# The decay sums of a forgetting attention as three float16 parts in two tiles, with new ranks for the planner

## The chip, the cores and the metric

The kernel runs on one core of one Trainium2 chip. The time is the device time of one execution in microseconds (us), from launch to end. The core has a matrix engine (TensorE: PE for its products, PEld for its weight loads), a vector engine (VectorE, DVE), an engine for functions of one input (ScalarE, ACT), a slower general engine (GpSimd, POOL), and a queue that issues DMA transfers (SyncE, SP). Each works through its own instructions in order; semaphores tie them together.

## The reference

Three layers in a row, all in float32. Only the attention is touched by the change.

```python
# B, H, S, D = 4, 8, 576, 64: 32 heads
scores = (1.0 / sqrt(D)) * (q @ k.T)
log_f = log(clip(f, 1e-4, 1.0))              # f: [B, H, S]
cum = cumsum(log_f, axis=-1)
scores = where(causal, -1e9, scores + cum[..., :, None] - cum[..., None, :])
attn = exp(scores - max(scores)); attn = attn / (sum(attn) + 1e-9)
x = attn @ v                                  # joined to [B, S, 512]
# token mixing over S (576 -> 256 -> 576), then channel mixing (512 -> 1536 -> 512)
u = x + (relu(x.T @ w_tok1) @ w_tok2).T
x = u + relu(u @ w_ch1) @ w_ch2
# gated layer: 512 -> 1024, a convolution of three taps over S, a sigmoid gate, 1024 -> 512
h = conv(relu(x @ w_in), conv_w); out = (h_in * sigmoid(h)) @ w_out
```

The softmax of a row is the same when a constant is added to it, so the term of the row (`cum[:, None]`) can be left out: the kernel adds only the column's term, the decay, to the scores.

## The kernel before, in words

The 32 heads are worked off in 16 pairs. One load `load_qk` brings q and k of a pair, one head in partitions 0 to 63 and the other in 64 to 127. `score` (L862 on) makes the scores of a pair in three sets of row blocks: block 4 (576 columns wide, two banks), blocks 0 and 3, blocks 1 and 2. A set is four products of q and k for the two heads (L885), and then two or four *decay products* (L889): a column of `sel`, repeated 128 times, selects the rows of `dec` that belong to the head and adds its decay to every row of the scores.

`smax` (DVE, L903) masks the scores and takes the row maximum, `sexp` (ACT, L909) the exponentials. Heads 0 to 7 and the last two are transposed by PE (`ptr`, L942), the others by a DMA, for which POOL makes a float16 high part and DVE a low part (`lo_part`, L924). `pv` multiplies by v (L974 in float32 for heads 0 to 7, L979 to L981 in float16 later). Four heads are a group; `t1` and `t2` mix the tokens of a group (`mm3`, L276 to L278; `t2_x`, L1119, transposes x). After two groups, u of a batch is scaled (`u_scale`), split into float16 high and low parts (`u_part`, low part at L508), and the first five blocks of the channel mixing can run (`channel_mix`: `m1` reads uh and ul, `rl` at L561 is its DVE part). These float16 products are the only large work of PE that needs no softmax, and they fill its gaps from then on.

Weights arrive packed; ACT (L313) and DVE (L317, L318) decode them, and DVE makes their low parts (L469, below called weight low part).

The decays come first of all. Four DMAs (L706) bring the whole of f, 32 rows, to each quarter of the partitions; DVE clips it (L712), ACT takes the logarithm (L713), DVE sums it (L714), and the sums are written as a rounded part and a remainder, two rows of fp32r per head, in both halves of the partitions (L718, L721). ACT copies pieces of `dec` to where the sets of blocks need them (L723).

What follows is put in order by a planner, the class `Order`. Every step is a task `T(engine, cost, rank, function, ...)` with the keys it reads and writes. The planner keeps a clock of its own and on each engine takes the task that can begin first, at equal times the one of lowest rank; the instructions are then emitted in that order, and each engine keeps it. So ranks, costs and the spacing of the heads (`PER`) set the order and nothing else. `SETR` and `LATER` are offsets of the ranks of the channel weights; `LATE` puts the channel products behind everything else.

## Time and profile before

| | |
|---|---|
| time, median of 3 runs | 727.55 us (725.85 to 730.85) |
| profiled execution | 727.58 us; span from first to last instruction 725.8 us |
| busy, share of the span | PE 97%, PEld 79%, DVE 69%, ACT 58%, POOL 30% |
| mean granted clock of TensorE | 0.988 |
| chain that ended last | PE 81%, DVE 7%, issue 6%, POOL 4% |

The span has 1.8 us around it that the profile doesn't show. A share of busy time is a mean over stages, and a matmul's record is longer than the time that it takes from the next one, because matmuls are pipelined. So PE at 97% says that PE nearly always has something in flight, not that it streams all the time; the stretches must be read one by one.

### The profile page before, as it was taken

The numbers are of one execution on the slowest core, as the hardware profiler recorded it, in microseconds if no ns is written. First come the engines' busy times: TensorE is split into PE (matmuls) and PEld (weight loads), VectorE is DVE, ScalarE is ACT, GpSimd is POOL, SyncE is SP. The second block draws the span as 40 slices with busy tenths as digits, with TensorE's granted clock in tenths as the row PEclk, the third lists the DMA queues.
The fourth block names the chain that finished last, engine by engine and source line by source line (L and its number), as shares of the span: only waits on it lengthen the run. The fifth ranks groups of instructions, "written<-read, shape, count | busy, mean of one in ns | idle before, by whom it ended". The sixth has DMA issues, their size and how long they took to land.

```text
span 725.8 us, 16282 instructions
## 1 busy us (share of the span) xinstructions
PE 706.5 (97%) x6412; PEld 573.8 (79%) x6412; DVE 502.8 (69%) x1225; ACT 420.8 (58%) x924; POOL 214.8 (30%) x270
## 2 busy tenths in 40 slices
...
GB/s 210 152 126 171 178 223 205 212 179 285 216 222 171 159 133 185 220 264 140 158 184 117 247 157 162 100 131 137 67 60 58 50 58 35 58 18 25 34 34 34
DMA packets 149581, 101.13 MB, mean 139 GB/s; under 512 B 86592, under 2 KB 141632, under 8 KB 149504
## 3 DMA queue, kind: packets, MB, share of 16 engines
...
q14 instruction: 27, 0.22, 0.1%
...
## 4 chain that ended last, share of the span: by engine, by line
PE 81%; DVE 7%; issue 6%; POOL 4%; ACT 1%; DMA 0%; SPq 0%; POOLq 0%; DVEq 0%; ACTq 0%
PE w L276 14%; PE w L277 14%; PE w L278 14%; PE z L277 7%; PE z L278 7%; PE z L276 7%; PE z L885 6%; PE w L974 3%; PE w L942 2%; POOL g L271 2%; PE z L889 2%; DVE pl L924 1%; PE w L1119 1%; PE w L980 1%; PE w L979 1%
## 5 line engine op out<-in xcount | busy, mean ns | idle before, releaser
L276 PEld LDWEIGHTS <-w 128*128 128x128 f16 x1280 | 125.4, 98 | 36.0 <-issue 4.5
L278 PEld LDWEIGHTS <-w 128*128 128x128 f16 x1280 | 125.5, 98 | 33.0 <-issue 1.1
L277 PEld LDWEIGHTS <-w 128*128 128x128 f16 x1280 | 125.3, 98 | 32.1 <-issue 1.1
L276 PE MATMUL w<-uh,w 128*128 128x288 f16 x416 | 119.8, 288 | 0.0
L278 PE MATMUL w<-uh,w 128*128 128x288 f16 x416 | 119.6, 288 | 0.0
L277 PE MATMUL w<-ul,w 128*128 128x288 f16 x416 | 119.6, 288 | 0.0
L1385 DVE SCALAR_TENSOR_TENSOR cv<-hp,cw,cv 128x286 f32<-128x286 f32 (+1 forms) x128 | 75.1, 593 | 43.4 <-ACT cv L1379 41.1
L271 POOL TENSOR_TENSOR g<-sg,g 128x286 f16<-128x286 f32 (+1 forms) x64 | 54.9, 863 | 156.1 <-ACT g L265 154.4
L909 ACT ACTIVATE t<-t,m 128x576 f32<-128x576 f32 (+4 forms) x160 | 81.7, 554 | 20.9 <-DVE m L903 18.5
L557 ACT ACTIVATE r<-w 128x288 f16<-128x288 f32 x96 | 39.0, 406 | 87.2 <-PE w L278 86.8
L903 DVE CUSTOM_DVE_ANT_0 t<-z,mask 128x576 f32<-128x576 f32 (+4 forms) x160 | 70.5, 479 | 17.9 <-PE z L889 17.8
L277 PE MATMUL z<-g,w 128*128 128x286 f16 (+1 forms) x256 | 73.3, 286 | 0.7 <-POOL g L271 0.7
L276 PE MATMUL z<-g,w 128*128 128x286 f16 (+1 forms) x256 | 73.0, 285 | 1.0 <-ACT g L265 1.0
L561 DVE SCALAR_TENSOR_TENSOR r<-w,r 128x288 f16<-128x288 f32 x96 | 43.4, 453 | 43.4 <-ACT r L557 43.2
L278 PE MATMUL z<-g,w 128*128 128x286 f16 (+1 forms) x256 | 72.9, 285 | 0.0
L634 POOL TENSOR_TENSOR p<-p,u 128x288 f32<-128x288 f32 x32 | 25.5, 828 | 152.1 <-DMA p<-p_d 151.3
L885 PE MATMUL z<-qk 64*128 64x288 f32 (+4 forms) x384 | 61.8, 432 | 7.0 <-DVE m L903 3.9
L271 POOL TENSOR_TENSOR xl<-xf,xh 128x320 fp32r<-128x320 f32 x32 | 34.0, 1064 | 110.2 <-ACT xh L265 110.1
L276 PE MATMUL w<-vh,w 128*128 128x288 f16 x224 | 64.1, 286 | 0.0
L277 PE MATMUL w<-vl,w 128*128 128x288 f16 x224 | 64.1, 286 | 0.0
L278 PE MATMUL w<-vh,w 128*128 128x288 f16 x224 | 64.1, 286 | 0.0
L276 PE MATMUL z<-r,w 128*128 128x288 f16 x224 | 64.1, 286 | 0.0
...
## 6 DMA issues: line engine op xcount, KB each, us to landing
...
qk<-in_qk_dram SPq DMA_DIRECT2D x16, 608.0 KB, 4.9
...
```

Source lines behind the costliest of these rows:

```text
L271: nc.gpsimd.tensor_tensor(o, a, b, ALU.subtract)
L276: nc.tensor.matmul(ps, wh, xh, start=(first and i == 0), stop=False)
L277: nc.tensor.matmul(ps, wh, xl, start=False, stop=False)
L278: nc.tensor.matmul(ps, wl, xh, start=False, stop=(last and i == n - 1))
L557: nc.scalar.activation(out=t[:, 0, :], in_=box["z", m], func=AF.Relu)
L561: nc.vector.scalar_tensor_tensor(t[:, 1, :], box["z", m], 0.0, f32(t[:, 0, :]), ALU.max, ALU.subtract)
L634: nc.gpsimd.tensor_tensor(box["p"][:, d], box["p"][:, d], box["u"][:, d], ALU.add)
L885: nc.tensor.matmul(out_[x], t[r, Q0[i]:Q0[i] + 128], t[r, k0:k0 + n], start=first, stop=False)
L903: nc.vector.tensor_tensor_reduce(to, z_t.pop((n, i)), mk, -0.125, 3e38, ALU.add, ALU.min, m_t[n][0:rows, i:i + 1])
L909: nc.scalar.activation(out=tt[0:rows, o:o + w], in_=tt[0:rows, o:o + w], func=AF.Exp, bias=m_t[n][0:rows, i:i + 1], scale=-1.0)
L974: nc.tensor.matmul(o[:, 0:65], p32(n)[:, 128 * blk:128 * blk + 128], vp32_t[g % 2][:, slot, hh, :], start=(j == 0), stop=(j == nb - 1))
L1385: nc.vector.scalar_tensor_tensor(cv, hp_t[m][:, s0 + t:s1 + t], cw[:, t, m:m + 1], cv, ALU.mult, ALU.add)
```

## The change

- **Parts.** The sum is written as three float16 parts in three rows of their own; with 16 heads to a tile there are two tiles, `dec_t[0]` for heads 0 to 15 and `dec_t[1]` for heads 16 to 31. Row r of a half holds part r // 16 of head r % 16. `less` is a column of -1 and 0 that subtracts the parts already written, so that each of the three needs the same four DVE instructions over all 128 partitions (`decay_parts`). `sel` has 16 columns, and both tiles use it.
- **Loads.** f comes by two DMAs, one to a tile, each repeating 16 rows eight times. The load of the first q and k stands between them.
- **Tables.** ACT fetches the table of the logarithm with a dummy instruction ahead of the data, and that of the exponential with another one directly after the two logarithms.
- **Second tile.** Its sum, parts and copies are planner tasks.
- **Numbers of the planner.** Costs, `PER`, `SETR`, `LATER` and the spacing of weights are changed.

```diff
@@ -204,9 +204,9 @@
     FULL = 2 * HG
     BY_PE = [n < FULL or n >= NH - 2 for n in range(NH)]
 
-    SETR = ((-5.0, 30.0),)
-    LATER = (-10.0, 20.0, 40.0)
-    PER = 6.0
+    SETR = ((5.0, 20.0),)
+    LATER = (-30.0, 20.0, 40.0)
+    PER = 6.5
 
     const = ctx.enter_context(tc.tile_pool(name="const", bufs=1))
     work = ctx.enter_context(tc.tile_pool(name="work", bufs=1))
@@ -469,7 +469,7 @@
                 nc.vector.scalar_tensor_tensor(t[:, 512:1024], WT[i], pw[:, 0:1], t[:, 0:512], ALU.mult, ALU.subtract)
 
             T("ACT", 0.75, cranks[k], high, reads=[("W", i), ("pw", name), *opened(j)], writes=[("W", j)])
-            T("DVE", 0.75, cranks[k], low, reads=[("W", i), ("pw", name)], writes=[("W", j)])
+            T("DVE", 1.0, cranks[k], low, reads=[("W", i), ("pw", name)], writes=[("W", j)])
         return pw
 
 
@@ -674,9 +674,10 @@
 
 
         DEC4, DEC12 = 128, S + 128
-        dec = ap1.tile([128, DEC12 + 512], F32R, name="dec", bufs=1)
-        dmain = dec[:, 64:64 + S]
-        sel = ap1.tile([128, NH], F32R, name="sel", bufs=1)
+        HB = NH // 2
+        dec_t = [ap1.tile([128, DEC12 + 512], F16, name=f"dec{a}", bufs=1) for a in range(2)]
+        sel = ap1.tile([128, HB], F16, name="sel", bufs=1)
+        less = ap1.tile([128, 2], F32, name="less", bufs=1)
 
         nc.gpsimd.memset(mask[:, 0:128], 0.0)
         warm = bank("z")
@@ -701,32 +702,58 @@
             v_t[g] = t
 
 
-        ft = ap1.tile([128, S], F32, tag="xh", name="ft")
-        for a in range(4):
-            nc.sync.dma_start(ft[NH * a:NH * a + NH], f)
-        load_qk(0)
-        zer = ap1.tile([128, S], F32, tag="xl", name="zer")
-        cum = ap1.tile([128, S], F32, tag="us", name="cum", bufs=2)
+
+
+
+        nc.vector.memset(ones, 1.0)
+        tiny = ap1.tile([128, 1], F32, name="tiny", bufs=1)
+        nc.scalar.activation(out=tiny, in_=ones, func=AF.Ln)
+        ft_t = [ap1.tile([128, S], F32, tag="xh", name="ft"), None]
+        cum_t = [ap1.tile([128, S], F32, tag="us", name="cum", bufs=2) for _ in range(2)]
+        ft_t[1] = cum_t[1]
+        for a in range(2):
+            nc.sync.dma_start(ft_t[a], f[HB * a:HB * a + HB].partition_broadcast(128 // HB))
+            if a == 0:
+                load_qk(0)
+        zer = ap1.tile([128, 1], F32, name="zer", bufs=1)
+        part = [ap1.tile([128, S], F16, tag="t1h", name="part"), ap1.tile([128, S], F16, tag="t1l", name="part")]
         nc.vector.memset(zer, 0.0)
         make_identity(nc, ident)
-        nc.vector.tensor_scalar(ft, ft, 1e-4, 1.0, ALU.max, ALU.min)
-        nc.scalar.activation(out=ft, in_=ft, func=AF.Ln)
-        nc.vector.tensor_tensor_scan(cum, ft, zer, 0.0, ALU.add, ALU.add)
-        for a in range(4):
-            r = slice(NH * a, NH * a + NH)
-            nc.vector.tensor_copy(sel[r], ident[r, NH * a:NH * a + NH])
-        nc.scalar.activation(out=dmain, in_=cum, func=AF.Copy, scale=-8.0)
-        for a in (1, 3):
-            r = slice(NH * a, NH * a + NH)
-            nc.vector.scalar_tensor_tensor(dmain[r], cum[r], -8.0, f32(dmain[r]), ALU.mult, ALU.subtract)
-        for a, n in ((DEC12 - 64, 64), (0, 64), (DEC12, WD[1]), (DEC12 + WD[1], WD[2])):
-            nc.scalar.activation(out=dec[:, a:a + n], in_=f32(dmain[:, 0:n]), func=AF.Copy)
+        own = ident.rearrange("p (x k h) -> p x k h", x=2, k=4)
+        nc.vector.tensor_reduce(less[:, 0:1], own[:, :, 0], mybir.AxisListType.XY, ALU.add)
+        nc.vector.tensor_scalar(less[:, 0:1], less[:, 0:1], 1.0, None, ALU.subtract)
+        nc.vector.tensor_reduce(less[:, 1:2], own[:, :, 2], mybir.AxisListType.XY, ALU.add, negate=True)
+        for a in range(2):
+            nc.vector.tensor_scalar(ft_t[a], ft_t[a], 1e-4, 1.0, ALU.max, ALU.min)
+            nc.scalar.activation(out=ft_t[a], in_=ft_t[a], func=AF.Ln)
+        nc.scalar.activation(out=tiny, in_=ones, func=AF.Exp)
+
+        def decay_sum(a):
+            nc.vector.tensor_tensor_scan(cum_t[a], ft_t[a], zer.to_broadcast([128, S]), 0.0, ALU.add, ALU.add)
+
+        def decay_parts(a):
+            cum, main = cum_t[a], dec_t[a][:, 64:64 + S]
+            nc.vector.tensor_copy(part[a], cum)
+            nc.vector.scalar_tensor_tensor(cum, part[a], less[:, 0:1], cum, ALU.mult, ALU.add)
+            nc.vector.tensor_copy(part[a], cum)
+            nc.vector.scalar_tensor_tensor(main, part[a], less[:, 1:2], cum, ALU.mult, ALU.add)
+
+        def decay_copies(a):
+            for at, n in ((DEC12 - 64, 64), (0, 64), (DEC12, WD[1]), (DEC12 + WD[1], WD[2])):
+                nc.scalar.activation(out=dec_t[a][:, at:at + n], in_=dec_t[a][:, 64:64 + n], func=AF.Copy)
+
+        decay_sum(0)
+        one = ap1.tile([128, HB], F32, name="one", bufs=1)
+        nc.vector.tensor_reduce(one, ident.rearrange("p (x k h) -> p h x k", x=2, k=4)[:, :, :, 0:3],
+                                mybir.AxisListType.XY, ALU.add)
+        nc.vector.tensor_scalar(sel, one, -8.0, None, ALU.mult)
+        decay_parts(0)
+        decay_copies(0)
 
         nc.gpsimd.memset(mask[:, 128:704], 0.0)
         nc.gpsimd.affine_select(
             out=mask[:, 512:640], in_=mask[:, 512:640], pattern=[[-1, 128]],
             compare_op=ALU.is_ge, fill=-8e9, base=0, channel_multiplier=1)
-        nc.vector.memset(ones, 1.0)
 
         TB = 4
         t_t = [ap2.tile([128, PW], F32, tag=f"t{i}", name=f"t{i}", bufs=1) for i in range(TB)]
@@ -885,8 +912,8 @@
                     nc.tensor.matmul(out_[x], t[r, Q0[i]:Q0[i] + 128], t[r, k0:k0 + n], start=first, stop=False)
             for out_, k0, n in sums:
                 for x, r in enumerate(halves):
-                    h = 2 * p + x
-                    nc.tensor.matmul(out_[x], sel[r, h:h + 1].to_broadcast([64, 128]), dec[r, k0:k0 + n],
+                    a, h = divmod(2 * p + x, HB)
+                    nc.tensor.matmul(out_[x], sel[r, h:h + 1].to_broadcast([64, 128]), dec_t[a][r, k0:k0 + n],
                                      start=False, stop=True)
 
         def smax(n, i):
@@ -1015,7 +1042,7 @@
         def x_lo(n):
             pool_sub(x_part(n, "xl"), x_of(n), f32(x_part(n, "xh")))
 
-        PE_S = {(4,): 1.42, (0, 3): 1.33, (1, 2): 1.28}
+        PE_S = {(4,): 1.45, (0, 3): 1.35, (1, 2): 1.2}
         DVE_S = {4: 0.81, 3: 0.69, 2: 0.56, 1: 0.42, 0: 0.29}
         ACT_E = {4: 0.78, 3: 0.67, 2: 0.56, 1: 0.46, 0: 0.34}
         SEG = ((4, 3), (2, 1, 0))
@@ -1028,7 +1055,7 @@
                 T("SP", 0.4, t0 - 9, load_qk, p, writes=[kq], moved=2.6, pools=A2)
             for blocks in SETS:
                 kz = [turn("z") for _ in range(2 if blocks == (4,) else 1)]
-                T("PE", PE_S[blocks], t0 + 1, score, p, blocks, reads=[kq], writes=[*kz, ("scores",)], pools=A2 + A1,
+                T("PE", PE_S[blocks], t0 + 1, score, p, blocks, reads=[kq] + [("dec", 1)] * (p >= HB // 2), writes=[*kz, ("scores",)], pools=A2 + A1,
                   ring=kz)
                 for x, i in ((x, i) for x in range(2) for i in blocks[::-1]):
                     n = 2 * p + x
@@ -1057,7 +1084,7 @@
                           writes=[("ptl", n % 2, a)], pools=A2 + ["a3"], ring=[kw])
                 else:
                     for q in range(2):
-                        T("POOL", (1.15, 0.8)[q], rank + 4, hi_part, n, q, reads=[(*kt, i) for i in SEG[q]],
+                        T("POOL", (1.22, 1.05)[q], rank + 4, hi_part, n, q, reads=[(*kt, i) for i in SEG[q]],
                           writes=[("ph", n % 2, q)], pools=A2)
                     T("SP", 1.5, rank + 5, transp, n, 0, reads=[("ph", n % 2, 0), ("ph", n % 2, 1)],
                       writes=[("pth", n % 2, a) for a in range(len(QUADS))], moved=2.5, pools=A3)
@@ -1075,7 +1102,7 @@
                 T("DVE", 0.5, rank + 6, norm, n, reads=[kw] + ([] if n < FULL else [("vsc", g % 3)]), writes=[("rs", n % 2)], pools=A1, ring=[kw])
                 T("DVE", 0.46, rank + 6, xout, n, reads=[kw, ("rs", n % 2)], writes=[("xf", g % 2, n % HG)], pools=A1, ring=[kw])
                 T("ACT", 0.45, rank + 6, x_hi, n, reads=[("xf", g % 2, n % HG)], writes=[("xh", n % HG)], pools=A1)
-                T("POOL", 0.9, rank + 6, x_lo, n, reads=[("xf", g % 2, n % HG), ("xh", n % HG)],
+                T("POOL", 1.05, rank + 6, x_lo, n, reads=[("xf", g % 2, n % HG), ("xh", n % HG)],
                   writes=[("xl", n % HG)], pools=A1)
 
 
@@ -1168,7 +1195,7 @@
                 kw = turn("w")
                 T("PE", 1.8, t0 + 3, t1, g, a, reads=[*xk, *W1K], pools=A1, ring=[kw],
                   writes=[kw, ("t1h", a), ("t1l", a)])
-                T("ACT", 0.37, t0 + 3, t1_hi, g, a, reads=[kw], writes=[("t1h", a)], pools=A1, ring=[kw])
+                T("ACT", 0.37, t0 + 3, t1_hi, g, a, reads=[kw, ("dec", 1)], writes=[("t1h", a)], pools=A1, ring=[kw])
                 T("DVE", 0.42, t0 + 3, t1_lo, g, a, reads=[kw, ("t1h", a)], writes=[("t1l", a)], pools=A1, ring=[kw])
             uk = [("us", g % 2, d, e) for d in range(NDM) for e in range(2)]
             for d in range(NDM):
@@ -1177,7 +1204,7 @@
                     first = d == 0 and e == 0
                     T("PE", 1.42, t0 + 4, t2, g, d, e, writes=[kw, *(uk if first else [("us", g % 2, d, e)])], pools=A1, ring=[kw],
                       reads=[(x, a) for x in ("t1h", "t1l") for a in range(KT)] + W2K + xf)
-                    T("ACT", 0.4, t0 + 4, u_copy, g, d, e, reads=[kw], writes=[("us", g % 2, d, e)], pools=A1, ring=[kw])
+                    T("ACT", 0.4, t0 + 4, u_copy, g, d, e, reads=[kw, ("dec", 1)], writes=[("us", g % 2, d, e)], pools=A1, ring=[kw])
             T("SP", 0.4, t0 + 5, u_out, g, reads=uk, writes=[("u_d", 2 * b, half), ("u_d", 2 * b + 1, half)],
               moved=2.4, pools=A1)
             T("DVE", 1.3, t0 + 4, u_largest, g, reads=uk, writes=[("um", b, half)], pools=A1)
@@ -1218,7 +1245,10 @@
         W1K = [("tokw", k) for k in range(3)]
         W2K = [("tokw", k) for k in range(3, 7)]
         v_tasks(0, -8)
-        AVAIL = [(H * (b + 1) - 1) * PER + 30 for b in range(B)]
+        T("DVE", 1.4, 16, decay_sum, 1, writes=[("dec", 1)], pools=["a1"])
+        T("DVE", 2.6, 22, decay_parts, 1, writes=[("dec", 1)], pools=["a1"])
+        T("ACT", 1.0, 24, decay_copies, 1, writes=[("dec", 1)], pools=["a1"])
+        AVAIL = [(H * (b + 1) - 1) * PER + 35 for b in range(B)]
         LATE = 1000.0
         for k, (block, hi, lo) in enumerate(tok_w):
             weight(block, lambda hi=hi, lo=lo: (hi, lo), 10 + 5.0 * k, ("tokw", k), pools_=["a1"])
@@ -1231,7 +1261,7 @@
                 q = t0 + SETR[x][y]
                 pw = weight_set(f"c{y + 1}{x}", [(name, m, (col_block if y == 0 else row_block)(w, m)) for m in ms],
                                 list(range(at, at + n)), at - 1 if at else 2 * M1,
-                                [q + 2.5 * k for k in range(n)], [q + 2.5 * n + 2.5 * k for k in range(n)], factor)
+                                [q + 2.0 * k for k in range(n)], [q + 2.0 * n + 2.0 * k for k in range(n)], factor)
                 if y == 0:
                     pws.append([pw])
                 else:
```

Where a name moved: L885, L889, L903 and L909 of before are L912, L916, L930 and L936 after the change; `mm3` keeps its lines.

Three places show how the order moves. The first is the beginning of DVE. `ft` (and in the changed kernel `cum`, for the second tile) holds f, L712 or L727 clips it, L714 or L732 sums it, L721 or L736 to L739 write the parts, and L903 or L930 is the first row maximum, of head 0. Before:

```order
L710 MEMSET zer 128x576
L712 TENSOR_SCALAR ft<-ft 128x576
L714 SCALAR_TENSOR_TENSOR cum<-ft,zer 128x576
L717 CAST sel<-ident 32x32 x4
L721 SCALAR_TENSOR_TENSOR dec<-cum,dec 32x576 x2
L729 MEMSET ones 128x1
L903 ISA t_182,m<-z,mask 128x576
```

Now:

```order
L727 TENSOR_SCALAR ft<-ft 128x576
L727 TENSOR_SCALAR cum<-cum 128x576
L732 SCALAR_TENSOR_TENSOR cum<-ft,zer 128x576
L747 TENSOR_REDUCE one<-ident 128x16
L749 TENSOR_SCALAR sel<-one 128x16
L736 CAST part<-cum 128x576
L737 SCALAR_TENSOR_TENSOR cum<-part,less,cum 128x576
L738 CAST part<-cum 128x576
L739 SCALAR_TENSOR_TENSOR dec_133<-part,less,cum 128x576
L732 SCALAR_TENSOR_TENSOR cum<-cum,zer 128x576
...
L930 ISA t_193,m<-z,mask 128x576
```

The clip of the second tile stands ahead of the first sum, and the second tile's sum and its four parts (the rows left out) stand ahead of head 0's maximum.

The second place is PE ahead of the scores of pair 4 (heads 8 and 9). L974 or L1001 is `pv` in float32, L1119 or L1146 the transposes of x for `t2`, L942 or L969 transposes attention weights. Before:

```order
L974 MATMUL w<-vp_195,pt 128x65 x10
L885 MATMUL z<-qk_148 128x288 x4
L889 MATMUL z<-dec,sel 128x288 x4
L1119 MATMUL w<-ident,xf 128x128 x3
L276 MATMUL w<-w2h,t1h 128x288
L277 MATMUL w<-w2l,t1h 128x288
L278 MATMUL w<-w2h,t1l 128x288
...
L942 MATMUL w<-ident,t_184 128x128 x12
```

Now:

```order
L1146 MATMUL w<-ident,xf 128x128 x3
L276 MATMUL w<-w2h,t1h 128x288
L277 MATMUL w<-w2l,t1h 128x288
L278 MATMUL w<-w2h,t1l 128x288
...
L1001 MATMUL w<-vp_206,pt 128x65 x15
L969 MATMUL w<-ident,t_195 128x128 x12
L912 MATMUL z<-qk_150 128x288 x4
```

Three transposes of x, the six products of `t2` that follow them, and twelve transposes of attention weights moved from behind the first scores of pair 4 to ahead of them.

The third place is DVE between heads 11 and 12, where the channel mixing of the first batch begins: `r<-w,r` is `rl` (L561), `ul` a low part of u (L508), L317 and L318 decode a weight. Before:

```order
L508 SCALAR_TENSOR_TENSOR ul<-us,su_73,uh 128x576 x3
L924 SCALAR_TENSOR_TENSOR pl<-t_185,ph 128x640
L561 SCALAR_TENSOR_TENSOR r<-w,r 128x288
L903 ISA t_182,m<-z,mask 128x576
...
L318 SCALAR_TENSOR_TENSOR w_119<-w_119,wraw 128x512
```

Now:

```order
L561 SCALAR_TENSOR_TENSOR r<-w,r 128x288 x2
L930 ISA t_196,m<-z,mask 128x192
...
L318 SCALAR_TENSOR_TENSOR w_120<-w_120,wraw 128x512
L561 SCALAR_TENSOR_TENSOR r<-w,r 128x288
L951 SCALAR_TENSOR_TENSOR pl<-t_196,ph 128x1024
L951 SCALAR_TENSOR_TENSOR pl<-t_196,ph 128x640
L561 SCALAR_TENSOR_TENSOR r<-w,r 128x288
L317 TENSOR_SCALAR wraw<-wraw 128x512
L318 SCALAR_TENSOR_TENSOR w_121<-w_121,wraw 128x512
L561 SCALAR_TENSOR_TENSOR r<-w,r 128x288 x2
L930 ISA t_193,m<-z,mask 128x576
```

Six `rl` stand ahead of head 12's first maximum (the last row) where there was one.

## Rows read from the trace of the kernel before

**Rows 1.** Windows, cut at the first 128x576 maximum of heads 2, 8, 14 and 24.

```profile
core 0: us, PE busy (x) PEld busy (x) DVE busy (x) ACT busy (x) POOL busy (x), PEclk, DMA share, GB/s
20.40:69.60 49.20, 49.20 (x406) 43.10 (x406) 32.62 (x109) 38.87 (x86) 18.25 (x23) 1.00 0.46 146
69.60:132.00 62.40, 55.41 (x534) 45.31 (x533) 57.80 (x145) 41.33 (x88) 34.08 (x34) 0.92 0.83 192
132.00:216.10 84.10, 83.20 (x922) 67.42 (x920) 76.37 (x209) 57.78 (x121) 45.74 (x43) 1.00 0.98 228
```

**Rows 2.** Windows of the stretches at half clock, and of a late one.

```profile
10.00:16.80 6.80, 5.83 (x24) 3.54 (x25) 2.90 (x11) 5.22 (x11) 0.72 (x1) 0.50 1.19 256
88.50:91.90 3.40, 3.40 (x18) 3.40 (x17) 3.37 (x9) 2.82 (x4) 1.87 (x3) 0.50 1.13 208
105.60:112.40 6.80, 5.80 (x24) 3.81 (x25) 6.80 (x10) 4.74 (x10) 4.29 (x3) 0.50 0.75 190
400.00:600.00 200.00, 200.00 (x1635) 159.89 (x1633) 128.92 (x276) 88.98 (x200) 41.12 (x49) 1.00 0.36 111
```

**Rows 3.** Timeline of the beginning: start, length, engine, instruction, idle time before it.

```profile
0.74 1.80 SPq L706 DMA_DIRECT2D ft<-in_f_dram  x4
...
2.58 0.42 SPq L690 DMA_DIRECT2D qk<-in_qk_dram  x1
...
4.24 0.55 DVE L712 TENSOR_SCALAR ft<-ft 128x576 f32<-128x576 f32 x1 [2.78 <-DMA ft<-in_f_dram]
...
6.22 1.36 DVE L714 TENSOR_TENSOR_SCAN cum<-ft,zer 128x576 f32<-128x576 f32 x1 [1.43 <-ACT ft L713]
...
8.32 1.53 DVE L721 SCALAR_TENSOR_TENSOR dec<-cum,dec 32x576 fp32r<-32x576 f32 x2
...
10.98 1.28 ACT L909 ACT_TABLE_LOAD   x1
11.02 0.76 DVE L903 CUSTOM_DVE_ANT_0 t<-z,mask 128x576 f32<-128x576 f32 x1 [1.04 <-PE z L889]
...
12.28 0.78 ACT L909 ACTIVATE t<-t,m 128x576 f32<-128x576 f32 x1
```

**Rows 4.** DMA issues of the first 3 us: KB each, us from issue to landing.

```profile
qk<-in_qk_dram SPq DMA_DIRECT2D x1, 608.0 KB, 4.6
ft<-in_f_dram SPq DMA_DIRECT2D x4, 72.0 KB, 2.0
```

**Rows 5.** DVE groups by form: busy us, mean ns of one, idle before.

```profile
L469 DVE SCALAR_TENSOR_TENSOR w<-w,pw_c,w 128x512 f16<-128x512 f32 x24 | 23.3, 970 | 2.6 <-ACT w L465 2.6
...
L508 DVE SCALAR_TENSOR_TENSOR ul<-us,su,uh 128x576 f16<-128x576 f32 x16 | 15.3, 993 | 0.0
...
L561 DVE SCALAR_TENSOR_TENSOR r<-w,r 128x288 f16<-128x288 f32 x96 | 43.4, 453 | 43.4 <-ACT r L557 43.2
...
L262 DVE TENSOR_REDUCE um<-us 128x1 f32<-128x1152 f32 x8 | 10.8, 1348 | 7.6 <-ACT us L265 7.6
...
L955 DVE COPY pt<-w 128x512 f32<-128x512 f32 x8 | 5.4, 683 | 1.5 <-PE w L942 1.3
...
L717 DVE CAST sel<-ident 32x32 fp32r<-32x32 f32 x4 | 0.7, 166 | 0.0
```

**Rows 6.** Timeline of PE: twelve transposes, then the first set of a pair.

```profile
31.59 1.48 PE L942 MATMUL w<-ident,t 128*128 128x128 f32 x12
...
49.53 1.24 PE L885 MATMUL z<-qk 64*128 64x288 f32 x8
50.39 0.64 PE L889 MATMUL z<-dec,sel 64*128 64x288 f32 x4
50.96 0.39 PE L276 MATMUL w<-xh,w1h 128*128 128x256 f32 x1
```

**Rows 7.** Weight loads by form: busy us, mean ns of one, idle before.

```profile
L276 PEld LDWEIGHTS <-w 128*128 128x128 f16 x1280 | 125.4, 98 | 36.0 <-issue 4.5 <-PE z L889 0.3
...
L889 PEld LDWEIGHTS z<-dec,sel 64*128 64x128 f32 x128 | 14.6, 198 | 7.8 <-issue 2.9 <-DVE dec L721 1.7 <-ACT t L909 0.4
```

## The prediction

> **What bounds the kernel now.** I read the windows first, cut where a head's first maximum begins, because the page's mean hides that two engines take turns. From head 2 to head 8 PE has something in flight all the time (49.20 of 49.20 us) and DVE is busy for 32.62: PE is the bound. From head 8 to head 14 it is the other way about: DVE 57.80 of 62.40, PE 55.41 and at a mean clock of 0.92. From head 14 to head 24 both are nearly full (83.20 and 76.37 of 84.10) [rows 1]. In a late stretch PE puts 1635 matmuls into 200.00 us without a gap, 0.122 us each; that is what a float16 product of 288 columns costs, not the length of its record [rows 2].
>
> So the end is set by PE: its work, and the time that it loses. It loses time in two places. One is the beginning, where nothing can start before the decays are there: head 0's first maximum begins at 11.02 [rows 3]. The other is between heads 8 and 14. An estimate of the work that stands in PE's order between them: 108 products of 256 or 288 columns at 0.122 (36 of the channel mixing, 42 of `t2`, 30 of `t1`), 41 transposes at 0.12 (1.48 for twelve) [rows 6], nine sets of scores at 1.43, the time from one to what follows it [rows 6], and some 195 short records of `pv`, which have no row here and get half of 0.122. That is 13.2 + 4.9 + 12.9 + 11.9 = 43 us, in 62.40: some 20 us are lost, because DVE is the bound and the channel mixing has hardly begun. Part of it is the clock, which stood at 0.50, the level of 1.2 GHz, from 88.5 to 91.9 and from 105.6 to 112.4 [rows 2].
>
> The wait at the beginning is a chain: four DMAs of f, issued from 0.74 to 2.54; the clip, which waited 2.78 us for them, at 4.24; the sum at 6.22, 1.36 long; the parts at 8.32, 1.53; the maximum at 11.02. The exponentials' table takes from 10.98 to 12.26, so the first exponential begins at 12.28 and not at the end of the maximum, 11.78 [rows 3].
>
> **The change, part by part.** *The loads.* Before, f is 288 KB and q and k of the first pair 608 KB; the last DMA of f was issued at about 2.1 and took 2.0, so f was there at 4.1, and q and k at 2.58 + 4.6 = 7.2 [rows 3, 4]. That is 608 KB in 3.1 us, 196 KB per us. Now f for heads 0 to 15 is one DMA of 288 KB. With 72 KB after 2.0 us and the other 216 at that rate it is there at 0.74 + 2.0 + 1.1 = 3.8, slightly earlier. Then q and k follow, 3.1 us, 6.9. Then the second f, 288 KB, 1.5 us: 8.4. The bytes ahead of head 0 have grown by 288 KB, since each tile is repeated eight times.
>
> *DVE's queue.* The order puts the second clip ahead of the first sum, and DVE goes in order: the first sum, ready at about 5, waits for the second f. It is followed by the two small instructions for `sel`, the four for the parts, then the second tile's sum and four parts, and only then by head 0's maximum. The clip is 0.55 and the sum 1.36 as before [rows 3]; a small instruction 0.17 (the cast) [rows 5]. A part is two casts and two instructions with three operands. No row has these shapes. For the cast I take 0.55 (the clip has the same size); it may be 0.17 at the least, the small cast. For the others 0.76, half of L721's 1.53; 0.99 at the most, L508, the same 576 columns to float16 [rows 3, 5]. So parts are 2.6, between 1.9 and 3.1.
> Sum: 8.4 + 0.55 + 1.36 + 0.34 + 2.6 + 1.36 + 2.6 = 17.2 against 11.02: **6.2 us later**. If the second f lands together with q and k and the parts are short: 6.9 + 0.55 + 1.36 + 0.34 + 1.9 + 1.36 + 1.9 = 14.3, 3.3 later. If the DMAs move a quarter less and the parts are long, 10.2 + 0.55 + 1.36 + 0.34 + 3.1 + 1.36 + 3.1 = 20.0, 9.0 later.
>
> *The tables.* Both are fetched while ACT waits anyway. The logarithm's gains nothing, as the sum waits for the second f. The exponential's no longer stands between maximum and exponential: 12.28 - 11.78 = **0.5 less**. The copies of both tiles (1 us each) lie in ACT's wait.
>
> *The clock at the start.* Before, it was 0.50 from 10.0 to 16.8 [rows 2], some 5 us of it with PE at work. Now PE idles longer, and works at the lower level for as long after its restart; I take no difference.
>
> *The decay products.* Their number and columns stay. In a set the first decay product starts 0.86 us after the first score product and the next work 0.57 after that [rows 6]; four products of 288 columns, two heads at a time, need 2 x 0.12 of streaming, and the wait for what follows is the rest. The loads of `sel` lie beside the score products, so I cost float16 in place of fp32r at nothing. It has two bounds: 128 loads of 0.198 become 0.098 [rows 7], 12.8 us gained if every one had been on the path; and if float16 loads of the two halves were no longer hidden, 128 x 0.098 = 12.5 us lost. The nearest row is the set in rows 6, where they are hidden.
> The Trainium skill speaks for the gain: by "TensorE: Matmul & The Clock Gate", section "Weight-path perf modes", weights that are not FP32 load in a faster mode when there are 128 of them. The trace agrees as to the loads, 98 ns against 198; by that rule alone, were loads on the path, the time would come out at rival 2 below.
>
> *The order up to head 8.* Here PE is the bound, and ahead of pair 4's scores it now has twelve transposes, three transposes of x and six products of `t2` more: 15 x 0.12 + 6 x 0.122 = **2.5 us later**.
>
> *The order from head 8 to head 24.* Here DVE is the bound. Counted between the first maxima of these two heads, its order now holds two weight low parts, one `rl`, one copy and one `largest` less: 2 x 0.97 + 0.45 + 0.68 + 1.35 = **4.4 us earlier** [rows 5]. The copy and the `largest` went ahead of head 8, where DVE has time; the low parts and `rl` behind head 24, where PE is the bound again. Up to head 24 PE has done three channel products less, **0.4** for later. PE's order between heads 8 and 14 now holds 84 channel products where it held 36. That fills part of the 20 us, but DVE sets the pace on to head 24, and between heads 14 and 24 PE then has 57 in place of 108: what it gains first it lacks afterwards.
>
> *The sum.* 6.2 - 0.5 + 2.5 - 4.4 + 0.4 = 4.2. The profiled execution took 727.58, 0.03 from the median: **731.8 us**. With the bounds of the start it is 728.9 to 734.6.
>
> **The rivals.** *1. The earlier channel products are worth more.* 48 of them, 48 x 0.122 = 5.9 us, moved into the stretch in which PE lacks work. If DVE doesn't bind between heads 14 and 24 after all (there it is busy for 76.37 of 84.10, so 7.7 us are free), the gain is kept: 731.8 - 5.9 = 725.9. If the two stretches at half clock go with it, 10.2 us of which half is lost, another 5.1 at the most: 720.8. For it speaks that PE, with work to do, wouldn't fall to 1.2 GHz; against it that DVE has the same work in sum. I give its time as **726**.
> *2. The float16 loads are worth something.* All of the 12.8 us on the path give **719**. Against it: the products in rows 6 wait for the score products and not for a load.
> *3. DVE waits at a place where it has no time, and it gets slower.* Six `rl` now stand ahead of head 12's maximum where one stood. Each needs twelve matmuls of PE, 1.47 us, and takes 0.45. If DVE reaches them before PE has made the products, all that is behind them in the queue waits, head 12's maximum and the low parts of the transposes first, and through the maxima PE itself: 6 x (1.47 - 0.45) = 6.1 us. That gives **738**. It decides when PE reaches the first of these products late, which a late beginning makes likelier; against it, weights' decodes and low parts stand between the `rl`, 5 us of other work.
> *4. The start is no longer than before.* That needs the second f by 2.3 us, before q and k and even before the first f of old (4.1): excluded by the bytes.
>
> **How the numbers follow.** The forecast gets 0.48, rival 1 0.22, rival 2 0.07, rival 3 0.23. A measurement of this kernel, whose three runs span 5 us, can tell about 1% from no change: 720.3 to 734.8. The forecast (728.9 to 734.6) lies within it, and most of rival 1. Faster by over 1% is rival 2 and the end of rival 1: 0.12. Slower by over 1% is most of rival 3 and the forecast's upper end: 0.23. The rest, 0.65, is no change. The range reaches from rival 1's end to a little beyond rival 3: 720 to 740; it leaves rival 2 and a start with both bounds against it together with rival 3.
>
> **What would show each step.** The second f lands at about 8.4 and the first sum of DVE begins then, though the first logarithm is done at about 5. Head 0's first maximum begins at about 17, head 8's at about 78 (69.6 before), head 24's at about 220 (216.1). Decay products and what follows them keep their spacing (0.57 in the set of rows 6). Between heads 8 and 14 DVE stays above 90% busy and PE loses less than 20 us; between 14 and 24 PE loses more than the 1 us in rows 1. I am wrong if the first maximum begins before 14, if head 8's shift isn't found again at head 24, or if PE shows waits after head 30, where the late stretch has none [rows 2]: that stretch I take as unchanged, though the ranks of the later weights moved too.

## The result, and the profile after

The changed kernel takes 735.13 us (median of 7 runs, 734.41 to 736.44), the kernel before 727.55 (7 runs): a ratio of 1.0093 over all their runs, interval 1.0069 to 1.0117, some 7 us slower (the medians alone lie 7.6 apart). That is within the range and 3.3 us over the forecast of 731.8. Its profiled execution took 735.13, the span 733.3.

The windows of the changed kernel, cut at the first maxima of heads 2, 8, 14 and 24 as [rows 1] are, and one of the three stretches that its trace has at half clock (columns as there):

```profile
28.10:78.30 50.20, 50.20 (x422) 43.99 (x423) 32.94 (x110) 39.88 (x89) 17.17 (x23) 1.00 0.44 141
78.30:143.50 65.20, 58.60 (x566) 46.66 (x565) 57.93 (x153) 43.51 (x90) 32.94 (x36) 0.95 0.81 192
143.50:221.70 78.20, 76.01 (x852) 59.32 (x853) 72.32 (x193) 53.69 (x111) 41.22 (x40) 0.98 1.02 228
...
92.20:95.60 3.40, 3.40 (x17) 2.36 (x14) 3.16 (x13) 2.10 (x3) 2.61 (x4) 0.50 0.33 69
```

What bounds each stretch is what bounded it before: PE up to head 8, DVE behind that. The stretches from head 2 to head 24 add up to 193.6 us against 195.7, so the 7 us are not there. They are ahead of them, but for 1.7 us between heads 24 and 30. The timeline of the beginning, engines SP, DVE and ACT (columns as in [rows 3]):

```profile
0.74 0.81 SPq L715 DMA_DIRECT2D ft<-in_f_dram  x1
1.60 0.41 SPq L691 DMA_DIRECT2D qk<-in_qk_dram  x1
2.07 0.64 SPq L715 DMA_DIRECT2D cum<-in_f_dram  x1
2.75 0.68 SPq L779 DMA_DIRECT2D vp<-in_v_dram  x1
...
5.97 0.46 DVE L727 TENSOR_SCALAR ft<-ft 128x576 f32<-128x576 f32 x1 [4.03 <-DMA ft<-in_f_dram]
...
10.93 0.46 DVE L727 TENSOR_SCALAR cum<-cum 128x576 f32<-128x576 f32 x1 [4.50 <-DMA cum<-in_f_dram]
11.31 1.35 DVE L732 TENSOR_TENSOR_SCAN cum<-ft,zer 128x576 f32<-128x576 f32 x1
...
18.78 0.82 DVE L739 SCALAR_TENSOR_TENSOR dec<-part,less,cum 128x576 f16<-128x576 f16 x1
19.52 0.75 DVE L930 CUSTOM_DVE_ANT_0 t<-z,mask 128x576 f32<-128x576 f32 x1
...
20.55 0.76 ACT L936 ACTIVATE t<-t,m 128x576 f32<-128x576 f32 x1
```

The reader is to see three times. The first clip waits for its f until 5.97; before, the clip began at 4.24 although its f came by four DMAs [rows 3]. The second clip, which the queue has ahead of the first sum, waits until 10.93, so the logarithm that was ready at about 7.1 lay for 4 us. Head 0's first maximum begins at 19.52 in place of 11.02, 8.5 us later. Head 8's begins at 78.26 (8.6 later than 69.62), head 24's at 221.70 (5.6 later than 216.06), head 30's at 268.85 (7.3 later than 261.54); the end of the span is 7.5 later.

The decay products are what they were. The first set of a later pair on PE's timeline (as [rows 6]), and the loads by form (as [rows 7]):

```profile
26.60 1.24 PE L912 MATMUL z<-qk 64*128 64x288 f32 x8
27.67 0.41 PE L916 MATMUL z<-dec,sel 64*128 64x288 f16 x4
28.01 0.66 PE L969 MATMUL w<-ident,t 128*128 128x128 f32 x4
```
```profile
L916 PEld LDWEIGHTS <-sel 64*128 64x128 f16 x128 | 7.6, 97 | 13.9 <-issue 6.5 <-DVE sel L749 3.7
```

A load of `sel` takes 97 ns in place of 198, and the set takes 28.01 - 26.60 = 1.41 us from its first score product to what follows, where it took 50.96 - 49.53 = 1.43. Half the load time, and nothing comes out.

### The profile page after: what moved, and what is told of

Its sections match the earlier page's. It is cut to its first block, busy times and chain, and to the rows that moved or that the text cites. A ratio compares the mean times of both kernels' runs of the same rounds, so it can differ in the third digit from the quotient of the medians.

```text
span 733.3 us, 16261 instructions
## 1 busy us (share of the span) xinstructions
PE 706.1 (96%) x6412; PEld 567.4 (77%) x6412; DVE 508.2 (69%) x1234; ACT 422.8 (58%) x930; POOL 206.6 (28%) x270
## 4 chain that ended last, share of the span: by engine, by line
PE 83%; DVE 5%; issue 5%; POOL 3%; DMA 1%; ACT 1%; SPq 0%; POOLq 0%; ACTq 0%; DVEq 0%
PE w L276 14%; PE w L277 14%; PE w L278 14%; PE z L277 7%; PE z L278 7%; PE z L276 7%; PE z L912 7%; PE w L1001 4%; PE w L1146 2%; PE w L969 2%; POOL g L271 2%; PE w L1006 1%; PE w L1007 1%; PE z L916 1%; PE w L1008 1%
## 5 line engine op out<-in xcount | busy, mean ns | idle before, releaser
L936 ACT ACTIVATE t<-t,m 128x192 f32<-128x192 f32 (+4 forms) x160 | 81.8, 553 | 16.6 <-DVE m L930 15.9
L930 DVE CUSTOM_DVE_ANT_0 t<-z,mask 128x192 f32<-128x192 f32 (+4 forms) x160 | 71.1, 479 | 11.2 <-PE z L916 11.1
L912 PE MATMUL z<-qk 64*128 64x288 f32 (+4 forms) x384 | 63.3, 440 | 10.8 <-DVE m L930 8.6
L561 DVE SCALAR_TENSOR_TENSOR r<-w,r 128x288 f16<-128x288 f32 x96 | 43.2, 453 | 42.9 <-ACT r L557 42.5
L276 PE MATMUL z<-r,w 128*128 128x288 f16 x224 | 64.1, 286 | 0.0
L277 PE MATMUL z<-r,w 128*128 128x288 f16 x224 | 64.1, 286 | 0.0
```

Of the source, the lines that this page charges most:

```text
L276: nc.tensor.matmul(ps, wh, xh, start=(first and i == 0), stop=False)
L277: nc.tensor.matmul(ps, wh, xl, start=False, stop=False)
L561: nc.vector.scalar_tensor_tensor(t[:, 1, :], box["z", m], 0.0, f32(t[:, 0, :]), ALU.max, ALU.subtract)
L912: nc.tensor.matmul(out_[x], t[r, Q0[i]:Q0[i] + 128], t[r, k0:k0 + n], start=first, stop=False)
L930: nc.vector.tensor_tensor_reduce(to, z_t.pop((n, i)), mk, -0.125, 3e38, ALU.add, ALU.min, m_t[n][0:rows, i:i + 1])
L936: nc.scalar.activation(out=tt[0:rows, o:o + w], in_=tt[0:rows, o:o + w], func=AF.Exp, bias=m_t[n][0:rows, i:i + 1], scale=-1.0)
```

## The experiments

The theory: the whole loss is the later start, and the rest of the change (float16, the new order) is worth nothing or a little. The rivals: the new order costs something in itself; or a later start is partly taken up between heads 8 and 14, where DVE is the bound. "Start" is where head 0's first maximum begins in the profiled execution. Ratios are to the kernel before, run on the same chip (728.7 to 728.9 us there, so 0.001 is 0.7 us). "New order" says that PE's 6,059 matmuls stand exactly in the changed kernel's order, and the other engines' instructions too but for the decays' own; "old order" the same of the kernel before. Edits are shown shortened.

| kernel | decays | order | start | ratio, interval |
|---|---|---|---|---|
| e1_defer | two tiles, the second later | another | 13.2 | 1.0064 (1.0043 to 1.0085) |
| e2_clip | two tiles, second clip later | new | 16.8 | 1.0063 (1.0038 to 1.0088) |
| e3_ranks | old | new numbers, nearly the new order | 11.0 | 1.0045 (1.0028 to 1.0061) |
| e4_parts | two tiles | old numbers, another order | 19.7 | 1.029 (1.0229 to 1.0351) |
| e5_four | two tiles, 4 + 4 DMAs | new | 25.7 | 1.017 (1.0149 to 1.0192) |
| e6_delay | two tiles, 10 clips more | new | 24.8 | 1.0139 (1.0124 to 1.0154) |
| e7_half | second tile left out | new | 12.1 | 0.999 (0.9978 to 1.0002) |
| e8_oldplan | two tiles | old | 19.7 | 1.0112 (1.0091 to 1.0133) |
| e9_one_sp | one float16 tile | new | 12.4 | 0.9981 (0.997 to 0.9992) |
| e10_one_two | one tile, two queues | new | 10.6 | 0.9973 (0.9959 to 0.9987) |
| e11_old_new | old | new | 10.8 | 0.9978 (0.9967 to 0.9989) |
| e12_one_old | one tile, two queues | old | 10.8 | 0.9992 (0.998 to 1.0004) |

**e1_defer: the second tile out of the way.**

```
 for a in range(2): dma ft_t[a]          # both ahead of load_qk(0)
 decay_log(0); decay_sum(0); decay_log(1)
-T("DVE", 1.4, 16, decay_sum, 1, ...)    # planned ahead of head 0
+if p == 0: T("DVE", 1.4, 16, decay_sum, 1, reads=[("m", n, i) for n in range(2) ...])
```

> The changed kernel with the start undone in time, not in work: the second f is issued ahead of q and k, its clip and logarithm stand behind the first sum, and the second tile's sum, parts and copies come behind the maxima of heads 0 and 1. Start theory (the whole loss is head 0's maximum at 19.5 in place of 11.0, carried to the end): the first maximum comes at about 12.8, 6.7 earlier than in the changed kernel, and the time is 728.5, with 727 to 730. Order theory (the new order after head 0 loses the time, and a late start would have been taken up by DVE's free time up to head 8): the time stays at 733 or above.

The start came 6.3 us earlier and the ratio fell only from 1.0093 to 1.0064, 2 us. Its 733.2 us are the order theory's number, its start the start theory's. Moving the tasks moved the planner: some 400 of 1,234 DVE instructions stand elsewhere than in the changed kernel. So the run changes two things, and by itself it looked as if most of an earlier start were eaten. In its trace head 30's first maximum still comes 7.3 earlier than in the changed kernel (261.53), and from there to the end it takes 469.8 us against 464.4: the other order leaves more work for the end. The later runs hold the order fixed.

**e2_clip: only the second clip and logarithm, behind the first tile's parts.**

```
-for a in range(2): clip ft_t[a]; log ft_t[a]
+decay_log(0)
 decay_sum(0); decay_parts(0)
+decay_log(1)
```

> The changed kernel with only the second tile's clip and logarithm moved behind the first tile's parts; the second f is still behind q and k, and the second tile's sum and parts still stand ahead of head 0's maximum. Start theory: the first sum begins at about 7.1 and not at 11.3, the first maximum at about 16.2, 3.3 earlier, and the time is 731.8, half of the way back. Order theory: 734 or above.

Start 2.7 us earlier, ratio 1.0063: 2.2 us less than the changed kernel, in the same order. For the start, though this size alone is inside the intervals.

**e3_ranks and e4_parts: the two halves of the change apart.** e3 is the kernel before with all the new numbers of the planner, e4 the changed kernel with all the old ones.

```
-SETR = ((-5.0, 30.0),); LATER = (-10.0, 20.0, 40.0); PER = 6.0
+SETR = ((5.0, 20.0),);  LATER = (-30.0, 20.0, 40.0); PER = 6.5     # and seven costs, AVAIL and
                                                                     # the weights' spacing; e4 the other way
```

> The kernel before, with its decays and loads, but with all the planner's numbers of the changed kernel (costs, spacing of heads, offsets of the weights). Start theory: the first maximum stays at 11.0, head 8 comes 2 to 3 later, head 24 is back to within 2, and the time is within 3 of the kernel before: 725 to 730. Order theory: 733 or above.

> The changed kernel's decays, loads and tables with all the planner's numbers of the kernel before. Start theory: the first maximum is at 19.5 as in the changed kernel, and the time 733 to 737. Order theory: 727 to 730.

Both expectations fail, and both in the same direction: either half alone is worse than thought. e4 lost 2.9%, 21 us. e3 ends between its two expectations, e4 beyond both of its own. The planner makes its order from both halves at once, so a half is a kernel in an order that nobody chose. e8 takes that apart.

**e8_oldplan: new decays, exactly the old order.** The second tile's sum, parts and copies are written out ahead of head 0, and the planner doesn't see them.

```
-T("DVE", 1.4, 16, decay_sum, 1, ...); T("DVE", 2.6, 22, decay_parts, 1, ...); T("ACT", ...)
+decay_sum(1); decay_parts(1); decay_copies(1)      # behind decay_copies(0); old numbers
```

> The new decays (two float16 tiles, one DMA each, both tables ahead) with exactly the order of the kernel before on PE and POOL, and on VectorE and ScalarE too but for the decays themselves; the second tile's sum and parts stand ahead of head 0. Differs from the kernel with new decays and old numbers (1.029) only in that the planner doesn't see the second tile's tasks. If that kernel's loss is an order that these tasks upset: 727.5 + 8.5 = 736 at the most, ratio 1.008 to 1.012, the same as the changed kernel, and the new numbers then only repair what the tasks upset. Rival: the old order doesn't stand a start that is 8.5 us later, whatever the tasks do (waits of VectorE between heads 8 and 14): 740 to 750, ratio over 1.017.

1.0112 against 1.029, with the same decays and the same start of 19.7. The 13 us between them are order alone: three tasks of 5 us in the planner's account, with the old numbers, upset it. Windows of e4 from head 8 to 14 and 14 to 24, then of e8 (columns as in [rows 1]):

```profile
79.80:141.50 61.70, 50.29 (x458) 38.48 (x459) 58.19 (x144) 39.31 (x82) 28.82 (x30) 0.92 0.77 196
141.50:230.60 89.10, 84.70 (x941) 65.91 (x939) 76.93 (x204) 58.14 (x120) 48.08 (x48) 0.96 0.94 210
```
```profile
77.40:141.50 64.10, 56.30 (x528) 44.31 (x527) 57.92 (x144) 40.74 (x86) 33.04 (x34) 0.89 0.80 190
141.50:226.10 84.60, 83.60 (x928) 66.03 (x926) 76.76 (x209) 57.94 (x122) 45.87 (x43) 1.00 1.00 224
```

In e4 PE has nothing in flight for 11.41 + 4.40 = 15.8 us of these stretches, in e8 for 7.80 + 1.00 = 8.8, with 1,399 matmuls done against 1,456: what it didn't do in the wait it does afterwards. DVE is busy for the same time in both. So the new numbers repair what the new tasks would upset; they don't pay for the start.

**e5_four and e6_delay: a later start, the same order.** e5 fetches each tile of f by four DMAs of 32 rows, two repeats each:

```
-dma(ft_t[a], f[16a:16a+16].partition_broadcast(8))
+for q in range(4): dma(ft_t[a][32q:32q+32], f[16a:16a+16].partition_broadcast(2))
```

> The changed kernel with each tile of f fetched by four DMAs of 32 rows (two repeats each) in place of one of 128 rows; the order on every engine is the same. If the one repeating DMA is what brought the first f late (5.95 us in place of the 4.1 of the kernel before), the first f lands at about 4.1, the first logarithm ends 1.9 earlier, and q and k follow at 7 to 8. But six more issues of 0.6 us stand on SP, so the second f, which the first sum waits for, lands at 9 to 11: head 0's first maximum at 18 to 20 and the time within 1 us of the changed kernel (ratio to before 1.008 to 1.011). Rival: the bytes count and not the number of DMAs, the first f lands at 6 again.

The first f came at 9.65 and not at 4.1 or 6, the second at 17.06, the start is 25.7. Both expectations are wrong. The DMA view shows what holds the landing up; here it is for e5 from 2.5 to 4.5 us, when nothing but f moves for most of the time (busy tenths of the core's 16 DMA engines, and GB/s, each in 40 slices):

```profile
DMA  0000000000011211111120211111120211111150
GB/s 0 0 0 0 0 0 0 0 0 0 0 46 46 92 46 46 46 46 46 46 92 0 92 46 46 46 46 46 46 92 0 92 46 46 46 46 46 46 92 0
```

One to two tenths of 16 engines are at work. Counted from start and duration of f's packets of 2,304 bytes, at most 3 are under way at a time in e5 (two repeats), 10 in the changed kernel (eight repeats) and 17 in the kernel before (no repeats); a packet takes 93 ns in the median in e5 and in the kernel before. So the packets are as fast, and fewer run side by side.

e6 delays the start and does nothing else:

```
 decay_parts(0); decay_copies(0)
+for _ in range(10): clip cum_t[0]       # nothing reads it any more
```

> The changed kernel with ten further clips of an array that nothing reads any more on VectorE, ahead of the second tile's sum: a pure delay of 10 x 0.46 = 4.6 us before head 0's first maximum (24.1 in place of 19.5). The order of all else is the same on every engine. Start theory: what the start loses is found in the end, 4.6 us, ratio to before about 1.0156. Rival (a part is taken up between heads 8 and 14, where VectorE is the bound; by the deferral experiment 2.0 of 6.3 come out): 1.5 us, ratio about 1.011.

Start 5.3 us later, ratio 1.0139: 3.4 us more than the changed kernel, between the two expectations. The order is that of the changed kernel, so the missing 1.9 us are no matter of order; at intervals of 1.1 us and 1.7 us it isn't settled that they are missing. The profiled executions say more. From head 0's first maximum to the end e2, e5 and e6 all take 712.4 us, with starts of 16.75, 25.65 and 24.83: a start that is up to 8.9 us later is found in full at the end. The changed kernel's profiled execution takes 713.8 for the same, and it loses between heads 8 and 24 (143.4 us against 141.4 in the three), where its granted clock fell to 0.50 for three times 3.4 us and theirs shows no fall.

**e7_half: without the second tile.**

```
-for a in range(2): dma, clip, log      -> range(1)
-T("DVE", 1.4, 16, decay_sum, 1, ...)
+T("DVE", 1.4, 16, lambda a: None, 1, ...)   # planned, does nothing
-dec_t[a][r, ...]  +dec_t[0][r, ...]
```

> Leaves out the second tile: its DMA of f, clip, logarithm, sum, parts and copies; heads 16 to 31 take their decay products from the first tile, the same number and shapes. The order of all that is left is the changed kernel's on every engine, unlike in the deferral experiment. Head 0's first maximum should begin at about 5.95 + 0.46 + 0.68 + 1.36 + 0.3 + 2.6 = 11.4 to 12.5, some 7 us earlier. Start theory: all 7 us come out, ratio to before 0.999 to 1.001, and so the rest of the change is worth nothing. Rival (a third comes out, the rest is waited for between heads 8 and 14): ratio about 1.006.

0.999: with the start back at 12.1 the loss is gone. (Heads 16 to 31 here use the decays of other heads, so the run is a test of time only.) This is the run that decides: everything else of the change is still there, order included, and in sum nothing of it costs. With e2 it also splits the 8.5 us of the start. The first tile alone is 1.1 later than before (12.12 against 11.02), the second tile's clip, sum and parts ahead of head 0 add 4.6 (e2, 16.75), and the wait for the second f ahead of the first sum adds 2.8 (19.52).

**e9_one_sp and e10_one_two: the three parts in one tile.** If the second tile is what costs, it can be spared. The decay product of head 2p + x reads 64 rows, half x, so half 0 needs the three parts of the even heads alone, 48 rows, and half 1 those of the odd ones.

```
-dma(ft_t[a], f[16a:16a+16].partition_broadcast(8)); a, h = divmod(2p + x, 16); sel[r, h], dec_t[a]
+heads_of = f.rearrange("(h x) s -> x h s", x=2)
+for k in range(4):
+    for x in range(2):
+        (SP if x == 0 else ACT).dma(ft_t[0][64x+16k : 64x+16k+16], heads_of[x])   # e9: SP for all
+sel[r, p], dec_t[0]
```

> A third arrangement: one float16 tile in place of two. Rows 0 to 63 hold the three parts of the 16 even heads, rows 64 to 127 those of the odd ones, since a product of head 2p + x reads only half x. f comes by eight DMAs of 16 rows with no repeating, all on SP ahead of q and k; sel is made before the clip. The order of all else is the changed kernel's. Eight issues of 0.46 us end at 4.4, so f lands at 5.5 to 6, and head 0's first maximum begins at 5.8 + 0.5 + 0.7 + 1.36 + 2.6 + 0.9 = 11.5 to 12.5, as in the kernel that left the second tile out: start theory 0.998 to 1.001 of before. Rival: q and k, now behind eight issues, come at 9 or later and the scores of head 0 end last; then the maximum begins at 12.5 or later, ratio over 1.001.

> The one tile again, with its eight DMAs of 16 rows split over two queues: four issued by SP and four by ScalarE, ahead of the logarithm's table there. If a DMA without repeating is spread over all 16 DMA engines, as the four of the kernel before, f lands at about 4.1, head 0's first maximum begins at 10.0 to 10.5, some 9.3 us earlier than in the changed kernel; at 0.96 us of time for each us of start (five kernels of the same order so far) that is ratio 0.996 to 0.998, ahead of both kernels. Rivals: ScalarE's issues or the table behind them hold up the logarithm (first maximum at 11.5 or later, ratio 0.999); or rows of 16 use fewer engines and f lands at 6 again.

e9: start 12.4, ratio 0.9981, both as expected. Its q and k came late (its first score product waits until 9.45), but the decay product is last. e10's beginning, timeline of SP, DVE, ACT and PE:

```profile
0.74 1.79 SPq L717 DMA_DIRECT2D ft<-in_f_dram  x4
...
4.42 0.46 DVE L733 TENSOR_SCALAR ft<-ft 128x576 f32<-128x576 f32 x1 [1.38 <-DMA ft<-in_f_dram]
4.92 0.68 ACT L734 ACTIVATE ft<-ft 128x576 f32<-128x576 f32 x1 [0.82 <-DVE ft L733]
...
5.63 1.36 DVE L738 TENSOR_TENSOR_SCAN cum<-ft,zer 128x576 f32<-128x576 f32 x1 [0.75 <-ACT ft L734]
...
8.87 0.82 DVE L745 SCALAR_TENSOR_TENSOR dec<-part,less,cum 128x576 f16<-128x576 f16 x1
...
9.74 0.71 PE L917 MATMUL z<-dec,sel 64*128 64x288 f16 x4 [1.28 <-DVE dec L745]
10.58 0.76 DVE L931 CUSTOM_DVE_ANT_0 t<-z,mask 128x576 f32<-128x576 f32 x1 [0.89 <-PE z L917]
```

f is there at 4.42, by DMAs that repeat nothing; at most 15 of its packets are under way at a time. The start is 10.6, just above what was expected, the ratio 0.9973 (0.9959 to 0.9987), inside it: faster than both kernels, by 2 us of the kernel before and 8.7 of the changed one.

**e11_old_new and e12_one_old: the other corners.** e11 is the kernel before in exactly the new order, by the new numbers and three planned tasks that do nothing; e12 is e10 in exactly the old order.

```
+T("DVE", 1.4, 16, lambda a: None, 1, ...)      # e11: and two more, and the new numbers
```

> The decays of the kernel before (one fp32r tile in two parts, no table ahead) with exactly the changed kernel's order on PE and POOL, and on VectorE and ScalarE but for the decays themselves: the fourth corner beside before (old, old), the changed kernel (new, new) and new decays with the old order. Start 11.0. If float16 products and the order are worth nothing, the time follows the start: the kernel that left the second tile out had 12.1 and 0.999, so 0.997 to 0.999 here, and the 1.0045 of the old decays with the new numbers lies in the few places where its order differs. Rival: the new order costs the old decays 0.4%, 1.003 to 1.006, so float16 products are worth 3 us in it.

> The one tile with its DMAs on two queues, and with exactly the order of the kernel before. First maximum at 10.0 to 10.5. From the two tiles in that order (19.7, 1.0112) 9.4 us earlier: 0.998 to 0.999, the same within 2 us as the one tile in the new order, if the order matters little once the start is the same. Rival: the new order is better for float16 by the 1.4 us between the two-tile kernels or more (0.9985 or above here against 0.997 there), or worse (below 0.996 here).

e11 meets its expectation. It differs from e3 in three planned tasks that do nothing and in the steps that the planner holds back for them, and so in the place of fewer than 50 matmuls on PE, and is 4.9 us faster. In the profiled executions the difference lies between heads 8 and 14 (64.2 us against 70.3, at a mean granted clock of 0.97 against 0.90); through which instructions stays open. e12's 0.9992 lies just above the 0.998 to 0.999 expected and fits the rival there, that the new order is the better one by 1.4 us. The rivals that give the order a cost, or float16 a gain, fall. Old against new order at the same decays: 1 to 0.9978 (old decays), 0.9992 to 0.9973 (one tile), 1.0112 to 1.0093 (two tiles), three times 0.0019 to 0.0022, some 1.5 us less. Only in the first pair do the runs tell the two apart (0.9967 to 0.9989 leaves out 1); in the other two the intervals overlap, and it is their agreement that speaks for the size. Old decays against float16 at nearly the same start: 0.9978 and 0.9973 in the new order, 1 and 0.9992 in the old, nothing that the intervals can tell. So the old decays in the new order are as fast as the best float16 version.

The eight kernels in the new order (the changed one, e2, e5, e6, e7, e9, e10, e11) have starts from 10.6 to 25.7 us. A straight line through ratio times 728.8 against the start rises by 0.93 us for each us, and none lies further than 1.1 us from it. That settles the second rival too, together with e2, e5 and e6 above: a later start is not taken up later on.

## Why the prediction came out as it did

The mechanism was right and the range held; **the start's term was too small**, the loads in it. Step by step:

*The loads.* Forecast: first f at 3.8, second f at 8.4. The clips began at 5.97 and 10.93. I had moved all bytes at the 196 KB per us of q and k, and said that one DMA of 288 KB would be slightly earlier than four of 72. But one that repeats 16 rows eight times keeps at most 10 packets under way where those kept up to 17 (e5, with two repeats, 3). And the second f's packets, from 6.80 to 9.81, took 3.0 us in place of the 1.5 forecast, 186 ns each in the median. They ran among the 256-byte packets of v, which had been issued right behind; but that is not shown to be the cause. In e1 the second f took 3.0 us, about 195 ns a packet, among the packets of q and k of 4,864 bytes, and in e5 its packets took 93 ns in spite of v's. The Trainium skill has the rule, "DMA: Bandwidth & Descriptors", section "Why a DMA increments its semaphore by 16 and not by 1": the engines that a DMA uses are the largest number up to 16 that divides the outermost dimension of both sides. By it e5 uses 2 engines, the changed kernel 8 and the kernel before 16, and the traces agree, with at most 3, 10 and 17 packets under way. Of the first f's 1.7 us, the first packet starts 0.5 later than before (2.29 against 1.77) and the last ends 1.1 later (4.88 against 3.79); why another 0.6 passes to the clip isn't settled.

*DVE's queue.* From the second clip to head 0's maximum I forecast 0.55 + 1.36 + 0.34 + 2 x 2.6 + 1.36 = 8.8; it is 19.52 - 10.93 = 8.6. So the whole error of the start, 8.5 for 6.2, is the landing of the second f. The start is inside the bound given (9.0), the landing isn't: that bound had the second f at 10.2, with longer parts. What the start costs is shown twice over: e7 and e10 take it away, and the changed kernel's loss goes with it.

*The tables.* Forecast 0.5 less. The first exponential begins 1.03 after the maximum's beginning in place of 12.28 - 11.02 = 1.26, so 0.2. e10 has them ahead and e11 hasn't, and their times don't differ.

*The decay products at nothing.* Right: 1.41 against 1.43 for a set, and e10 against e11. Both bounds, 12.8 less and 12.5 more, and rival 2 with them, are excluded by the intervals.

*The order.* The forecast had 2.5 later at head 8, 4.4 earlier up to head 24 and 0.4 later by three products: 1.5 earlier in sum. By the ratios it is some 1.5 earlier, so the sum held. Where it comes from can be read from three pairs of kernels that differ in the order alone. The first 128x576 maximum of a head on DVE's timeline, and the end of the span, in us:

| kernel | decays | order | head 0 | head 2 | head 8 | head 24 | head 30 | end |
|---|---|---|---|---|---|---|---|---|
| before | old | old | 11.02 | 20.41 | 69.62 | 216.06 | 261.54 | 725.8 |
| e11 | old | new | 10.76 | 19.19 | 69.52 | 212.78 | 260.13 | 724.6 |
| e12 | one tile | old | 10.82 | 19.86 | 68.87 | 214.82 | 260.13 | 726.1 |
| e10 | one tile | new | 10.58 | 19.74 | 69.90 | 210.95 | 258.10 | 722.7 |
| e8 | two tiles | old | 19.73 | 28.39 | 77.41 | 226.06 | 271.37 | 737.6 |
| changed | two tiles | new | 19.52 | 28.11 | 78.26 | 221.70 | 268.85 | 733.3 |

Two of its rows as the timeline has them, head 8's and head 24's first maxima in e11:

```profile
69.52 0.76 DVE L903 CUSTOM_DVE_ANT_0 t<-z,mask 128x576 f32<-128x576 f32 x1 [0.74 <-PE z L889]
212.78 0.76 DVE L903 CUSTOM_DVE_ANT_0 t<-z,mask 128x576 f32<-128x576 f32 x1 [0.39 <-PE z L889]
```

From head 2 to head 8 the new order takes 1.1 us more in each pair: the added transposes and products do cost, but 1.1 and not 2.5. From head 8 to head 24 it takes 3.2, 4.9 and 5.2 less, around the 4.4. From head 24 to head 30 it takes 1.8 to 1.9 more, where the forecast had 0.4. So the three terms are of the right sign, and that the sum came out as exactly as it did is luck: the first was 1.4 too large, the last 1.4 too small. These are single executions, and kernels of the same order differ by 2 us between heads 8 and 24 (e6, above); the ends of the three pairs lie 1.2, 3.4 and 4.3 us apart, so the size of the whole is taken from the ratios. Which instructions fill the wait ahead of head 8 wasn't tried.

Head 8's maximum, forecast at about 78 and found at 78.26, is a hit of the same kind: the start was 2.3 later than forecast, the transposes 1.4 cheaper, and from head 0 to head 2 the changed kernel took 8.6 us where the kernel before took 9.4. From head 30 to the end it is 464.4 against 464.3, so the late stretch is unchanged, as the forecast took it.

*The clock at the start.* The profile's windows give the changed kernel 1.00 up to 28 us, but its trace has no record of the clock ahead of 23.9, and the length of the products says otherwise. The first score products of the changed kernel, then the same eight in e6, which stand in a window at 0.50 there:

```profile
7.94 2.29 PE L912 MATMUL z<-qk 64*128 64x288 f32 x8 [1.89 <-DMA qk<-in_qk_dram]
8.28 2.29 PE L914 MATMUL z<-qk 64*128 64x288 f32 x8 [3.17 <-DMA qk<-in_qk_dram]
```

Eight of them take 1.24 at 26.60. So the changed kernel too worked at the lower level, from 7.94 at the latest to about 23.9, longer than the 6.8 us of before. "No difference" held all the same: most of that time was a wait, and from head 0 to head 2 nothing was lost. Between heads 8 and 24 the level fell for three times 3.4 us, against 3.4 and 6.8 before.

*Rival 1*, that the earlier channel products are worth 5.9 us, is excluded: the order gives 1.5. Its count was too high as well. The first of the three products of `m1` between the first maxima of heads 8 and 14, before and in the changed kernel (PE by form, columns as in [rows 5]):

```profile
L276 PE MATMUL w<-uh,w 128*128 128x288 f16 x30 | 9.3, 311 | 0.0
L276 PE MATMUL w<-uh,w 128*128 128x288 f16 x36 | 11.1, 308 | 0.9 <-ACT uh L505 0.9
```

That is about 90 channel products before and 108 now, 18 more and not 48: the forecast's 36 and 84 are counts of PE's order, and not of what PE did between the two maxima. With the trace's counts (also 240 short records of `pv`, 60 products of `t1` and `t2`, 44 transposes) and the forecast's own prices, PE's work there is an estimated 51 us and not 43, so some 11 of the 62.4 us were lost before, and not 20.

*Rival 3*, that DVE waits at the `rl`, is excluded too. DVE's waits from head 8 to head 14 in the changed kernel (line waited at, releaser: us in all, times, longest):

```profile
DVE t L930 <- PE z L916: 1.0, 2, 0.7
DVE r L561 <- ACT r L557: 0.8, 1, 0.8
```

One `rl` waits 0.8, where the rival had 6.1, and e11 is not slower. DVE is busy for 57.93 of 65.20 there, 89% and not above 90; between heads 14 and 24 PE has nothing in flight for 2.2 us (0.9 before), as forecast.

In sum: 8.5 x 0.93 = 7.9 for the start, less 1.5 for the order, is 6.4; measured 7.6 between the medians, and 0.0093 of 727.55 is 6.8.
